# Four small moves in a tuned attention-plus-MLP kernel: last output part in another buffer, one of w_out's four sums by an adding transfer, the verdict in the second batch, x's differences a pair sooner

## The chip, the cores and the metric

The kernel runs on one core of a Trainium2 chip. The metric is the device time of that core in microseconds (us). Every execution quoted here, of every kernel, was in the undisturbed (fast) state: one core alone, at a mean granted TensorE clock (the share of full speed that the chip granted) of 0.992 to 0.999. Times inside a trace count from the start of its span. The span is shorter than the device time of the same execution (895.2 against 897.08 us in the profiled run of the kernel before). In the lines of the profiler, PE is TensorE, DVE VectorE, ACT ScalarE and POOL GpSimd; SPq and ACTq are transfers issued by SyncE and ScalarE; L with a number is a line of the kernel; "issue" is time in which nothing that the profile shows was waited for.

## The reference, cut to what matters

```python
# attention: B=4, H=8, S=768, D=64; proj has 6 columns
mask   = bucket(q) == bucket(k)                 # sign bits of q @ proj, k @ proj
scores = where(mask, q @ k.T / 8, -1e9)
attn   = softmax(scores) @ v                    # float32
x      = attn.transpose(0, 2, 1, 3).reshape(3072, 512)
# MLP: w_in 512 x 2048, w_out 2048 x 512, alpha one value per hidden unit
h      = x @ w_in
g      = maximum(h, 0) + alpha * minimum(h, 0)
out    = g @ w_out                              # float32
```

## The kernel before

First come sixteen pairs of heads (some 340 us), then the MLP in four batches. In each batch eight blocks f_0 to f_7 form g from x and w_in, and seven blocks z form the output. Both layers use a scheme of seven block products in place of eight, so that sums and differences of blocks of x, g and the weights must be made beside the matmuls, most of them by VectorE. A block of the first layer takes TensorE 9.03 us.

Four places are touched.

**w_out's sums.** The second layer needs four combinations of the quarters of w_out. They are made once, in the f blocks of the first batch, in eight pieces n = 0 to 7: GpSimd's queue loads a piece (four planes of 128x256, 512 KB), VectorE makes four sums in place, and GpSimd's queue stores the piece. Two pieces share one tile wo. The wo tiles and the weight tiles wl of the second layer share one buffer of two slots:

```python
def load_w2(b, n):                     # weights of the second layer
    t = late[0].tile([P, NI, 2 * H2], F32, name=f"wl{b}_{n}", tag="wl")      # same two slots
    m = SIDES[ORDER[n]][0]
    nc.sync.dma_start(t, w_out_r[m] if m < 3 else w_out_s[(2, 0, 3, 1)[m - 3]])
    ...
def load_out(n):
    if n % 2 == 0:
        w_o[n] = late[0].tile([P, 2, 4, DM // 2], F32, name=f"wo{n}", tag="wl")
    nc.gpsimd.dma_start(w_o[n - n % 2][:, n % 2], w_out_r[:, :, n].rearrange("m p d -> p m d"))

def sum_out(n):
    w = w_o[n - n % 2][:, n % 2]
    for to, x, op, y in ((2, 3, ALU.add, 2), (3, 0, ALU.subtract, 3), (0, 2, ALU.subtract, 0), (1, 1, ALU.subtract, 0)):
        do(DVE.tensor_tensor(w[:, to], w[:, x], w[:, y], op=op))
    nc.gpsimd.dma_start(w_out_s[:, :, n].rearrange("m p d -> p m d"), w)
...
# j is the number of the block
for n_out in [(), (0,), (1,), (2, 3), (4,), (5, 6), (7,)][j] if j < 7 else ():
    sum_out(n_out)
for n_out in [(1,), (2, 3), (4,), (5, 6), (7,)][j] if j < 5 else ():
    load_out(n_out)
```

So the slot goes from hand to hand: pieces 4 and 5 may be loaded when the stores of 0 and 1 have landed, pieces 6 and 7 when those of 2 and 3 have, the first weight tile wl when those of 4 and 5 have. `do(...)` pins an instruction to the program's order on its engine. The transfers of load_out and sum_out are not pinned, so the scheduler chooses their order on GpSimd's queue.

**The last output tile.** Its two copies by VectorE go into a tile of the ring "o", whose older slot is still being stored:

```python
def turn_last(n):
    ...
    o = late[0].tile([P, 2, P, 2], F32, name=f"o_{p}", tag="o")
    ...
    do(DVE.tensor_copy(o[:, :, :, 0], ps))                                    # tx
    do(ACT.copy(o2.rearrange("p f i -> p i f"), ps2))                         # ty
    nc.scalar.dma_start(dst[:, 2], o2.rearrange("p f i -> p (f i)"))
    do(DVE.tensor_copy(o[:, :, :, 1], cells("tz", [(0, 1), (1, 1)])))
    nc.sync.dma_start(dst[:, :2], o.rearrange("p t f i -> p t (f i)"))        # the last store
```

**The verdict.** In the fifth f block of the first batch, three reductions over saved magnitudes (`largest`), a transposition by TensorE and nine tiny VectorE instructions (`verdict`) set a flag that tells whether the fast path was admissible. **x's differences.** Four subtractions of 128x768 make the combinations of x for the first batch, after pairs 12 to 15.

## Time and profile before

| | before |
|---|---|
| median of 3 runs | 895.83 us (895.3 to 896.73) |
| span of the profiled run | 895.2 us |
| TensorE busy | 883.6 us (99%) |
| VectorE busy | 756.2 us (84%) |
| idle of TensorE after its start, before its last transposition | 1.7 us in the three longest waits |
| from the start of the last transposition (tz, 886.50) to the end of the span | 8.7 us |

TensorE is the bound, and the idle time is all there is to win: the prediction below shows its waits and the end. The middle of the first batch: this is GpSimd's timeline there (start, duration, engine, source line, operation, tiles, count; in brackets how long the engine had stood idle and what released it); L957 are the loads, L964 the stores:

```profile
375.02 1.50 POOL L957 DMA_DIRECT2D wo<-w_out_r  x2 [5.26 <-DMA w_out_s<-wo]
378.04 0.76 POOL L964 DMA_DIRECT2D w_out_s<-wo  x1 [1.52 <-DVE wo L963]
379.75 0.76 POOL L964 DMA_DIRECT2D w_out_s<-wo  x1 [0.96 <-DVE wo L963]
387.71 1.50 POOL L957 DMA_DIRECT2D wo<-w_out_r  x2 [7.21 <-DMA w_out_s<-wo]
...
396.91 0.76 POOL L964 DMA_DIRECT2D w_out_s<-wo  x1 [6.95 <-DVE wo L963]
```

These are loads 4 and 5, stores 2 and 3, loads 6 and 7, and store 5. Both load pairs wait for stores, the stores wait only for VectorE's sums. The corresponding lines of VectorE's timeline show the eight additions of pieces 5 and 6 without any wait, and the first sum of the second layer (ws) with a short one:

```profile
394.81 3.51 DVE L963 TENSOR_TENSOR wo<-wo 128x256 f32<-128x256 f32 x8
...
409.10 0.69 DVE L979 TENSOR_TENSOR ws<-wl 128x512 f32<-128x512 f32 x1 [0.40 <-DMA wl<-w_out_r]
```

### The profile page before, as it was taken

The numbers are of one execution on the slowest core, as the hardware profiler recorded it, in microseconds if no ns is written. First come the engines' busy times: TensorE is split into PE (matmuls) and PEld (weight loads), VectorE is DVE, ScalarE is ACT, GpSimd is POOL, SyncE is SP. The second block draws the span as 40 slices with busy tenths as digits, with TensorE's granted clock in tenths as the row PEclk, the third lists the DMA queues.
The fourth block names the chain that finished last, engine by engine and source line by source line (L and its number), as shares of the span: only waits on it lengthen the run. The fifth ranks groups of instructions, "written<-read, shape, count | busy, mean of one in ns | idle before, by whom it ended". The sixth has DMA issues, their size and how long they took to land.

```text
span 895.2 us, 15372 instructions
## 1 busy us (share of the span) xinstructions
PE 883.6 (99%) x5886; PEld 595.2 (66%) x5886; DVE 756.2 (84%) x1266; ACT 407.2 (45%) x726; POOL 46.2 (5%) x109
## 2 busy tenths in 40 slices
PE   9999999999999999999999999999999999999996
PEld 5544445555555445557997557997557997557996
DVE  5888998989989997899898678988668988668985
ACT  6888888888888862222112222112222112222111
POOL 0000000100100001210000000000000000000000
PEclk9999999999999999999999999999999999999999
DMA  8565586686796726587334434333425242520241
GB/s 224 139 169 136 160 233 165 173 240 194 205 284 177 231 61 218 174 287 284 137 106 131 140 123 153 131 122 104 167 101 177 102 152 83 174 96 0 95 159 57
DMA packets 124978, 140.17 MB, mean 157 GB/s; under 512 B 77776, under 2 KB 109024, under 8 KB 121312
## 3 DMA queue, kind: packets, MB, share of 16 engines
q1 hardware_dynamic: 116368, 123.90, 43.9%
q0 software_dynamic: 6384, 14.29, 6.5%
q10 hardware_dynamic: 2144, 0.92, 0.4%
q8 instruction: 48, 0.79, 0.3%
q14 instruction: 34, 0.28, 0.1%
HBM read 104.87 MB, written 28.31 MB: 149 GB/s over the span
## 4 chain that ended last, share of the span: by engine, by line
PE 90%; DVE 4%; DMA 3%; issue 2%; ACT 1%; SPq 1%; POOL 0%; DVEq 0%; ACTq 0%; POOLq 0%
PE sc L734 17%; PE av L770 13%; PE f_0a L870 2%; PE z_5a L870 2%; PE z_6a L870 2%; PE z_3a L870 2%; PE f_1a L870 2%; PE f_2a L870 2%; PE z_7a L870 2%; PE z_2a L870 2%; PE f_3a L870 2%; PE z_4a L870 2%; PE z_1a L870 2%; PE f_5a L870 2%; PE f_7a L870 2%; PE f_4a L870 2%
## 5 line engine op out<-in xcount | busy, mean ns | idle before, releaser
L737 ACT ACTIVATE pt<-sc 128x768 f32<-128x768 f32 x192 | 154.9, 812 | 38.4 <-PE sc L734 37.9
L734 PE MATMUL sc<-qT,kT 64*128 64x384 f32 x768 | 155.2, 483 | 0.0
L770 PE MATMUL av<-pt,vn 128*32 128x385 f32 (+1 forms) x1536 | 127.4, 487 | 0.0
L770 PEld LDWEIGHTS av<-pt,vn 128*32 128x32 f32 x1536 | 48.9, 109 | 70.9 <-issue 70.0
L734 PEld LDWEIGHTS sc<-qT,kT 64*128 64x128 f32 x768 | 68.2, 188 | 39.5 <-issue 39.3
L923 DVE TENSOR_TENSOR g<-g,g 128x384 f32<-128x384 f32 x128 | 68.4, 555 | 2.2
L734 PE MATMUL sc<-qb,kb 64*128 64x384 bf16 x384 | 63.3, 324 | 0.3 <-DVE kb L719 0.2
L987 DVE TENSOR_TENSOR gs<-g,gs 128x768 f32<-128x768 f32 x56 | 53.3, 952 | 1.0
L987 DVE TENSOR_TENSOR gs<-g 128x768 f32<-128x768 f32 x56 | 53.3, 952 | 0.0
L979 DVE TENSOR_TENSOR ws<-wl 128x512 f32<-128x512 f32 x56 | 38.5, 688 | 17.4 <-DMA wl<-w_out_s 15.9
L919 DVE SCALAR_TENSOR_TENSOR g<-h,alpha 128x384 f32<-128x384 f32 x32 | 19.7, 616 | 26.1 <-ACT h L912 26.1
L734 PEld LDWEIGHTS <-kb 64*128 64x128 bf16 x384 | 19.0, 94 | 27.7 <-issue 4.3
L745 DVE TENSOR_TENSOR accp<-pt,pt 128x1536 f32<-128x1536 f32 x16 | 28.1, 1758 | 10.5 <-ACT pt L737 10.5
L712 ACT ACTIVATE qb<-hs,hb 32x384 bf16<-32x384 f32 x60 | 34.4, 573 | 1.1 <-PE hs L704 0.2
L752 DVE TENSOR_TENSOR accd<-accd,pt 128x1536 f32<-128x1536 f32 x16 | 28.1, 1759 | 1.7
L751 DVE TENSOR_TENSOR accd<-pt,pt 128x1536 f32<-128x1536 f32 x16 | 28.0, 1752 | 0.0
L759 DVE TENSOR_TENSOR accd<-accd,accp 128x1536 f32<-128x1536 f32 x16 | 28.0, 1748 | 0.0
L723 ACT ACTIVATE kb<-hs,hb 64x384 bf16<-64x384 f32 (+1 forms) x45 | 26.0, 577 | 0.6
L870 PE MATMUL f_0a<-x,wi 128*128 128x384 f32 x64 | 23.5, 490 | 0.0
L870 PE MATMUL f_5a<-x,wi 128*128 128x384 f32 x64 | 23.3, 487 | 0.0
L870 PE MATMUL f_7a<-x,wi 128*128 128x384 f32 x64 | 23.3, 487 | 0.0
L870 PE MATMUL f_2a<-x,wi 128*128 128x384 f32 x64 | 23.3, 487 | 0.0
(351 smaller groups left out, 1776.8 us busy)
## 6 DMA issues: line engine op xcount, KB each, us to landing
wi<-w_in_s SPq DMA_DIRECT2D x32, 896.0 KB, 4.7
wl<-w_out_s SPq DMA_DIRECT2D x16, 1024.0 KB, 4.8
wl<-w_out_r SPq DMA_DIRECT2D x12, 1024.0 KB, 4.8
raw<-in_moe_w_out_dram SPq DMA_DIRECT2D x16, 512.0 KB, 4.6
raw<-in_moe_w_in_dram SPq DMA_DIRECT2D x16, 512.0 KB, 4.3
w_in_s<-wsi SPq DMA_DIRECT2D x16, 448.0 KB, 5.5
vn<-in_v_dram SPq DMA_DIRECT2D x16, 384.0 KB, 4.5
x_s<-x SPq DMA_DIRECT2D x16, 384.0 KB, 4.3
```

Source lines behind the costliest of these rows:

```text
L712: do(ACT.activation(bits["q", pi][D * s : D * s + 32, cols], ps["q"][c : c + 32, 0 if engine is DVE else half, :CW], AF.Sign, bias=hb[c : ...
L734: do(PE.matmul(sc[:, s, :CW], what["k", pi][r, ks], what["q", pi][r, qs], start=first, stop=not first,))
L737: do(ACT.activation(pts[kc][:, g, :, :CW], sc[:, :, :CW], AF.Exp, scale=SCALE / DOWN))
L745: do(DVE.tensor_tensor(accp[pi], p(0), p(1), op=ALU.add))
L751: do(DVE.tensor_tensor(accd[pi], p(3), p(4), op=ALU.add))
L752: do(DVE.tensor_tensor(accd[pi], accd[pi], p(5), op=ALU.add))
L759: do(DVE.tensor_tensor(accd[pi], accd[pi], accp[pi], op=ALU.add))
L770: do(PE.matmul(av[pi][D * s + t : D * s + t + 32, g, :w], nat["v", pi][:, s, kc * D + t : kc * D + t + 32], pts[kc][:, g, s, :w], start=(k ...
L870: do(PE.matmul(self.ps[bank], self.left(left, k), self.right(right, k), start=start and k == 0, stop=k == self.nk - 1, skip_group_check=no ...
L923: do(DVE.tensor_tensor(new_g(b, to)[:, i], g_m[b, x][:, i], g_m[b, y][:, i], op=ALU.subtract))
L979: do(DVE.tensor_tensor(t, w2[b, n, x], w2[b, n, y], op=op))
L987: do(DVE.tensor_tensor(t, g2[b, n, x], g2[b, n, y], op=ALU.subtract))
```

## The change

It moves the last output tile into a buffer that has long been free. It lets the transfer that brings plane 3 of each piece of w_out a second time add it onto plane 2 on the way, so that VectorE makes three sums in place of four. It moves the verdict to the second batch, in which no sums of w_out are made. It makes x's differences after pairs 11, 12, 13 and 15.

```diff
         if n % 2 == 0:
             w_o[n] = late[0].tile([P, 2, 4, DM // 2], F32, name=f"wo{n}", tag="wl")
-        nc.gpsimd.dma_start(w_o[n - n % 2][:, n % 2], w_out_r[:, :, n].rearrange("m p d -> p m d"))
+        w = w_o[n - n % 2][:, n % 2]
+        nc.gpsimd.dma_start(w, w_out_r[:, :, n].rearrange("m p d -> p m d"))
+        nc.gpsimd.dma_start(w[:, 2], w_out_r[3, :, n], accum_op=ALU.add)
@@
-        for to, x, op, y in ((2, 3, ALU.add, 2), (3, 0, ALU.subtract, 3), (0, 2, ALU.subtract, 0), (1, 1, ALU.subtract, 0)):
+        for to, x, op, y in ((3, 0, ALU.subtract, 3), (0, 2, ALU.subtract, 0), (1, 1, ALU.subtract, 0)):
@@
-        o = late[0].tile([P, 2, P, 2], F32, name=f"o_{p}", tag="o")
+
+        o = late[0].tile([P, 2, P, 2], F32, name=f"o_{p}", tag="ws3")
@@
-            load_x(0, *{9: (0,), 10: (1, 3), 12: (2,)}[pi])
-        if pi >= 12:
-            sum_x(0, pi - 12, DVE)
+            load_x(0, *{9: (0,), 10: (2, 3), 12: (1,)}[pi])
+        if 11 <= pi < 14 or pi == 15:
+            sum_x(0, min(pi - 11, 3), DVE)
@@
-        if j == 4:
+        if (b, what, n) == (1, "1", 1):
             largest()
@@
-        if j == 4:
+        if (b, what, n) == (1, "1", 3):
             verdict()
```

## The prediction

> **What bounds the kernel now.** I read the busy table first, then TensorE's waits, then the chain of waits at the end and around the largest holes, and last the timelines there. The busy table settles the scale:
>
> ```profile
> PE 883.6 (99%) x5886; PEld 595.2 (66%) x5886; DVE 756.2 (84%) x1266; ACT 407.2 (45%) x726; POOL 46.2 (5%) x109
> ```
>
> TensorE is busy for 883.6 of a span of 895.2 us. The change adds or removes no matmul, so all it can touch is the remaining 11.6 us. TensorE's waits divide the inner part of it:
>
> ```profile
> PE nil L514 <- DVE hb L518: 1.2, 1, 1.2
> PE z_2c L870 <- DVE m L1008: 0.8, 1, 0.8
> PE sm L784 <- DVE accd L759: 0.6, 1, 0.6
> PE vd L1087 <- DVE top L1083: 0.3, 1, 0.3
> ```
>
> The first is the start. The other three are the verdict at 383 us, the second product of the first batch at 425 us, and the sums of pair 14 at 319 us: 1.7 us together. The rest, 8.3 us, lies after the last transposition of TensorE (886.94 us). The chain of waits and the timeline of the end show:
>
> ```profile
> 884.93 0.43 SPq L1040
> 885.36 0.04 issue
> 885.40 3.00 DMA out_dram<-o
> ```
>
> ```profile
> 888.44 0.43 DVE L1068 COPY o<-tx 128x256 f32<-128x256 f32 x1 [2.00 <-DMA out_dram<-o]
> 888.78 0.41 DVE L1071 COPY o<-tz 128x256 f32<-128x256 f32 x1
> 889.23 0.40 SPq L1072 DMA_DIRECT2D out_dram<-o  x1
> ```
>
> The last copy is ready for its input at 886.4 us, but its tile o is a slot whose previous contents are still being stored by twelve small transfers. VectorE sits 2.00 us for that. The last store follows at 889.23 us and lands 3.1 us later.
>
> The second place is the middle of the first batch, where w_out's sums pass through a tile that shares its slots (wl) with the weights of the second layer. The chain of waits there:
>
> ```profile
> 396.91 7.00 DMA w_out_s<-wo
> ...
> 404.25 4.83 DMA wl<-w_out_r
> 409.07 0.02 issue
> 409.10 0.70 DVE ws L979
> ```
>
> So the first weight load of the second layer waits for a store of w_out's sums (issued 396.91, landed 403.91), and VectorE cannot go on before 409.10. From there VectorE's timeline is gapless to 425.05, when it releases the bank for z_2c. TensorE's start there is thus the landing plus 16.0 us, however early TensorE comes.
>
> **What the Trainium skill says.** "DMA: Bandwidth & Descriptors", section "SWDGE vs HWDGE vs iDMA", says an accumulating DMA must be issued by GpSimd, so the eight new ones share POOL's queue with the loads and stores of the same tiles. Section "Anatomy of one DMA — SWDGE (gpsimd) path" says DMA engines do not wait on semaphores: the issuing sequencer waits before dispatch. The trace agrees: POOL waits 12.5 us for two stores before it issues loads, and everything behind stands. The same section gives 2.0 us + bytes/436e3; for 512 KB that is an estimate of 3.2 us. The trace shows a median of 7.2 us for the loads (3.8 us the quickest), because section "Issuing engines are not separate DMA queues" of that page applies: all queues interleave on the same 16 engines, and each 9.03 us block brings an 896 KB weight load. "PSUM — Partial Sum Buffer", section "Engine vs sequencer instructions", says VectorE's queue is strict FIFO, so a sum that waits for an adding transfer holds all of VectorE's later work.
>
> **The change, part by part.**
>
> Last part to a free place: the second last-store tile moves to ws3, whose older slot was last read a block earlier. The copy then follows VectorE's own m at 886.44: 0.43 us to 886.87. The second copy needs tz, 886.94: about 886.98 to 887.39. The issue is at about 887.42 instead of 889.23, a gain of 1.8 us. By then the 128 KB store on ScalarE's queue, issued at 886.95, is in flight, so I count 1.7 us.
>
> Verdict later: TensorE's f_4a starts at 381.79 and four matmuls take 1.29, so f_5a could start at 383.08; it starts at 383.67. The loss is 0.59 us, and VectorE spends about 0.25 + 1.4 us there while it is already late. In the second batch there are no sums of w_out, and the reductions are two blocks ahead of the transposition: I charge 0.1 us. But the 0.59 us does not count by itself: TensorE meets VectorE at z_2c anyway, so it only makes that wait longer unless VectorE or the load is earlier too.
>
> x's differences: four of 0.95 us, all still there, now after pairs 11, 12, 13, 15 instead of 12, 13, 14, 15. Pair 14's wait of 0.6 us comes out of VectorE's own run from 304.53 to 319.13, which begins when exp frees it (a gap of 0.35 us before accp). Pair 13 ends with one difference in both kernels, so this wait stays. After pair 11 VectorE had 1.7 us idle, which takes the extra 0.95. Value: 0.
>
> One sum by an adding transfer: eight additions of 0.43 us leave VectorE, 3.4 us, in blocks of the first layer where it is 86 to 96% busy. In exchange POOL's order becomes load, adding transfer (after the load's landing), store. The adding transfers of the attention part move 384 KB and land after 4.3 us at the quickest; for 128 KB I estimate 3 us from that. The compiled order puts the store of sum 2 behind adding transfers 4 and 5, the store of sum 4 behind adding transfer 6, and that of sum 5 behind 7. I followed the clock with durations of before. Store 1 goes at 368.2, lands about 374; loads 4 and 5 at 374.2 and 375.0, land about 378 and 379.5 to 383; stores 2 and 3 leave at 380.5 to 384 (before 378.04 and 379.75), land 387.5 to 391; loads 6 and 7 land 394 to 399 (before 394.6 and 396.1). Adding transfer 6 leaves at 394 to 397 and lands at 397 to 401. VectorE wants it at about 395.6, in front of six g's that TensorE needs for f_7b at 404. So VectorE, which finished these sums at 398.24 before, finishes them between 397 and 402. Store 5 leaves at 397 to 400 (before 396.91); wl lands at 408.5 to 412.5 (before 409.07). Whichever is later moves the 16.0 us run: minus 1 to plus 4 us, with the middle at plus 0.6.
>
> Sum: 895.8 − 1.7 (end) + 0.1 (verdict in the second batch) + 0.6 (middle of the first batch) + 0 (x) = 894.8.
>
> **The rivals.** First, everything works: no adding transfer is late, the load of wl lands a little sooner because VectorE reaches sum 5 some 2 us earlier, and the 1.9 us that TensorE loses between 383 and 425 (0.59, and 1.3 around z_2) go. That makes 895.8 − 1.7 − 1.9 = 892.2. For it speaks that VectorE's lateness is real; against it that the load waits for a transfer, not for an addition.
>
> Second, POOL's queue becomes the bound: one weight load of 896 KB cuts into load 5, as before, when it took 9.1 us, every later step comes 4 us later, and VectorE stands at sum 6. It makes 895.8 − 1.7 + 4.5 = 898.6. For it speaks the order on POOL and the long landings; against it that each store is only half as late by the time of the next, since the weight loads pace them.
>
> Third, the last store is not sooner, because it meets the stores still in flight (384 KB issued at 885.38, landed 888.2). Then 1 us of the 1.7 is lost: 895.8. Against it: its data begin only at about 888.9 if the delay of before (889.23 to 890) or somewhat more holds, when those are done.
>
> **Range and chances.** I give the first rival 0.35, the middle course 0.4, the second 0.25, and lean slightly to the good side: 894.7, with 892.2 to 898.6 for 8 in 10. 2% is 17.9 us, more than the whole idle time of TensorE, so faster by 2% is all but impossible; slower by 2% would need a stall of 20 us, which only a transfer chain far longer than any seen here would make.
>
> **What would show it.** In the changed profile: the copy o<-tx at about 886.5 with no wait for a store, the last issue at about 887.4; no wait of TensorE for top; the wait of sm unchanged at 0.6; VectorE's wait for an adding transfer at the sums of the sixth block; and ws of the first batch at 408 to 413, with the wait of z_2c moved with it. If there is no wait for the adding transfers and ws begins before 408, I was too dark; if VectorE stands at several sums, too bright. Waits of TensorE in the later batches would mean that I missed something.

## The result, and the profile after

The kernel became slower: a median of 902.09 us (901.35 to 903.17, six runs) against 896.37 us (895.3 to 896.93, six runs of the kernel before, the three early ones among them). The ratio is 1.0066, with a 95% interval of 1.0054 to 1.0079. Here and below a ratio is that of the mean times of fast runs of the same rounds (the figures come out when the first, profiled, execution of each kernel is left out), so it is not quite the ratio of the medians. The time lies above the predicted range (892.2 to 898.6), though inside 2%.

VectorE lost 3.3 us of work (752.9 us busy in place of 756.2), and the span still grew by 5.0 us, to 900.2. TensorE's waits in the profile after (us in total, times, longest) say where:

```profile
PE f_7b L870 <- DVE f_6p L915: 5.1, 1, 5.1
PE nil L514 <- DVE hb L518: 1.2, 1, 1.2
PE z_2c L870 <- DVE m L1010: 0.8, 1, 0.8
PE sm L784 <- DVE accd L759: 0.6, 1, 0.6
```

The wait for the verdict (vd) is gone, those of sm and z_2c are as they were, and a new one of 5.1 us stands at the first batch's last f block. TensorE's timeline shows it, and a second effect behind it:

```profile
401.87 1.45 PE L870 MATMUL f_6a<-x,wi 128*128 128x384 f32 x4
408.41 2.93 PE L870 MATMUL f_7b<-x,wi 128*128 128x384 f32 x4 [5.09 <-DVE f_6p L915]
411.13 1.82 PE L870 MATMUL f_7c<-x,wi 128*128 128x384 f32 x4
```

After the hole the same four matmuls take 2.93 and 1.82 us in place of 1.45: the granted clock was 0.72 from 408 to 414 us. That is what the Trainium skill warns of in "TensorE: Matmul & The Clock Gate", section "HAM oscillation — how this bites in real kernels", for idle gaps of TensorE over some 3.4 us, and the trace agrees. Here it cost nothing by itself: VectorE was the later of the two until z_2c, and its timeline shows no wait for TensorE between 404.36 and there.

TensorE waited because VectorE did. VectorE's timeline after, where L965 are the sums of w_out (three per piece now):

```profile
393.44 1.34 DVE L965 TENSOR_TENSOR wo<-wo 128x256 f32<-128x256 f32 x3
400.97 0.43 DVE L965 TENSOR_TENSOR wo<-wo 128x256 f32<-128x256 f32 x1 [6.19 <-DMA wo<-w_out_r]
404.36 0.88 DVE L965 TENSOR_TENSOR wo<-wo 128x256 f32<-128x256 f32 x2 [2.96 <-DMA wo<-w_out_r]
...
415.07 0.68 DVE L981 TENSOR_TENSOR ws<-wl 128x512 f32<-128x512 f32 x1
```

Piece 5 is summed at 393.44. Piece 6 then makes VectorE wait 6.19 us for its load (its first remaining sum needs planes 0 and 3 only) and another 2.96 us for its adding transfer. In the kernel before, piece 6 had landed by the time it was wanted. The addition f_6p, which empties the bank that f_7b writes, comes behind it. And ws begins at 415.07 in place of 409.10, 6.0 us later, without waiting for wl itself.

GpSimd's timeline after tells why piece 6 came so late (L958 loads, L959 adding transfers, L966 stores):

```profile
374.58 1.50 POOL L958 DMA_DIRECT2D wo<-w_out_r  x2 [5.80 <-DMA w_out_s<-wo]
379.49 0.91 POOL L959 DMA_DIRECT2D wo<-w_out_r  x1 [3.41 <-DMA wo<-w_out_r]
384.54 0.87 POOL L959 DMA_DIRECT2D wo<-w_out_r  x1 [4.13 <-DMA wo<-w_out_r]
385.10 1.88 POOL L966 DMA_DIRECT2D w_out_s<-wo  x2
394.61 1.50 POOL L958 DMA_DIRECT2D wo<-w_out_r  x2 [7.63 <-DMA w_out_s<-wo]
401.14 0.91 POOL L959 DMA_DIRECT2D wo<-w_out_r  x1 [5.03 <-DMA wo<-w_out_r]
...
403.34 1.17 POOL L966 DMA_DIRECT2D w_out_s<-wo  x1
```

Loads 4 and 5 start as early as before (374.58). But stores 2 and 3, which left at 378.04 and 379.75 before, now stand behind adding transfers 4 and 5, and adding transfer 5 waits until load 5 has landed, at about 384.2. So these stores leave at 385.10, loads 6 and 7 at 394.61 in place of 387.71, and add 6 can leave only at 401.14, when load 6 has landed. It lands at 404.27. That is the chain of waits of this stretch: load, landing, add, landing, store, landing, next load. Each link was there before except the adding one, which puts one more landing into each turn.

There is a second limit close behind the first. Store 5, which frees the slot of wl, leaves at 403.34 in place of 396.91. The first load of wl leaves SyncE's queue after that:

```profile
408.86 0.32 SPq L947 DMA_DIRECT2D wl<-w_out_r  x1
```

It took 5.6 us, so it landed at about 414.5, only 0.6 us before VectorE, itself late, asked for it.

From z_2c on both traces run alike: z_2c starts 5.95 us later than before, tz 6.03 us later (892.53 against 886.50), and the span ends 5.0 us later. So the new end is 1.0 us shorter than the old one. Its timeline:

```profile
892.39 0.42 DVE L1071 COPY o<-tx 128x256 f32<-128x256 f32 x1
...
893.00 0.42 DVE L1074 COPY o<-tz 128x256 f32<-128x256 f32 x1 [0.20 <-PE tz L1056]
894.27 0.39 SPq L1075 DMA_DIRECT2D out_dram<-o  x1
```

Neither copy waits for a store any more, as intended. But the last store leaves 0.85 us after its last copy ended (893.42). The waits of SyncE name what held it:

```profile
SPq L1075 <- DMA out_dram<-o: 2.0, 1, 2.0
```

It waits for another store, one that doesn't touch its tile. The compiled program counts the landings of all transfers of SyncE and ScalarE, loads too, on a set of eight semaphores, taken in turn (this is read from the built program, not from a trace). The turn of the last store falls on the semaphore of ScalarE's 384 KB store (issued at 891.40, landed 2.8 us later, at 894.2). In the kernel before that same wait existed, but the copy's own wait for the buffer (to 888.40) hid it.

### The profile page after: what moved, and what is told of

Same layout as the page of the kernel before. It is cut to its first block, busy times and chain, and to the rows that moved or that the text cites.

```text
span 900.2 us, 15377 instructions
## 1 busy us (share of the span) xinstructions
PE 884.9 (98%) x5886; PEld 595.3 (66%) x5886; DVE 752.9 (84%) x1258; ACT 407.1 (45%) x726; POOL 53.6 (6%) x117
## 4 chain that ended last, share of the span: by engine, by line
PE 51%; DMA 3%; issue 3%; DVE 3%; POOL 1%; POOLq 0%; DVEq 0%
PE z_4a L870 2%; PE z_7a L870 2%; PE z_3a L870 2%; PE z_6a L870 2%; PE z_5a L870 2%; PE z_2a L870 2%; DMA wo<-w_out_r 2%; PE z_1a L870 2%; PE f_4a L870 2%; PE f_7a L870 2%; PE f_6a L870 2%; PE f_5a L870 2%; PE f_3a L870 2%; PE f_2a L870 2%; PE f_1a L870 2%
## 5 line engine op out<-in xcount | busy, mean ns | idle before, releaser
L870 PE MATMUL f_1a<-x,wi 128*128 128x384 f32 x64 | 23.3, 486 | 0.0
L870 PE MATMUL f_3a<-x,wi 128*128 128x384 f32 x64 | 23.3, 486 | 0.0
```

The costliest lines, as they stand in the source:

```text
L870: do(PE.matmul(self.ps[bank], self.left(left, k), self.right(right, k), start=start and k == 0, stop=k == self.nk - 1, skip_group_check=no ...
```

## The experiments

Theory at the start: the whole loss comes from the adding transfers, through their place in GpSimd's order (T1); the end gained about 1.0 us, and the rest of the predicted 1.7 is the shared semaphore; verdict and x are worth half a microsecond or nothing. Rivals: the adding transfer's own way is too long in any order (R1); another part of the change, or several together, cause the loss (R2); the last store meets others in flight whatever it waits for (R3). All twelve results were correct. The runs came in three sets of rounds, each with its own executions of the kernel before: e1, e2, e3 and e7; e4, e6, e8 and e9; e5, e10, e11 and e12. In the table, "before" is the median of the kernel before in the same rounds. Each trace is of one execution: those of e1, e2, e8 and e11 are the slowest of their kernels (896.55, 903.64, 902.02 and 904.80 us), those of e6, e7 and e12 the fastest.

| run | what it is | median (range) | before | ratio (95%) |
|---|---|---|---|---|
| e1_tail | before + end | 895.18 (894.71–896.55) | 896.31 | 0.9985 (0.9972–0.9998) |
| e2_add | before + adding transfers | 902.06 (898.51–903.64) | 896.31 | 1.0056 (1.0040–1.0071) |
| e3_no_add | after − adding transfers | 895.13 (894.21–896.03) | 896.31 | 0.9985 (0.9972–0.9998) |
| e7_lane | e1 + other semaphore | 895.33 (894.69–895.76) | 896.31 | 0.9988 (0.9975–1.0001) |
| e4_verdict | before + verdict | 896.34 (895.34–896.67) | 896.67 | 0.9993 (0.9979–1.0007) |
| e6_add4 | after, adds for pieces 0–3 only | 894.64 (894.21–895.23) | 896.67 | 0.9977 (0.9964–0.9991) |
| e8_pinned | after, GpSimd's order by hand | 900.30 (899.72–902.02) | 896.67 | 1.0040 (1.0025–1.0056) |
| e9_sooner | e3 + piece 5 a block sooner | 894.46 (893.75–894.88) | 896.67 | 0.9972 (0.9959–0.9986) |
| e5_x | before + x | 896.35 (896.00–896.77) | 896.10 | 1.0003 (0.9990–1.0016) |
| e10_not6 | after, no add for piece 6 | 899.98 (895.46–901.28) | 896.10 | 1.0028 (1.0007–1.0050) |
| e11_later | after, pieces 6 and 7 summed together later | 901.65 (896.13–904.80) | 896.10 | 1.0049 (1.0030–1.0067) |
| e12_both | e9 + e7's edit | 894.18 (893.38–894.44) | 896.10 | 0.9979 (0.9966–0.9992) |

### The parts one by one

**e2_add**: only the adding transfers, onto the kernel before.

```diff
+        nc.gpsimd.dma_start(w[:, 2], w_out_r[3, :, n], accum_op=ALU.add)
-        for to, x, op, y in ((2, 3, ALU.add, 2), (3, 0, ...), (0, 2, ...), (1, 1, ...)):
+        for to, x, op, y in ((3, 0, ...), (0, 2, ...), (1, 1, ...)):
```

> The kernel before with the adding transfers alone. Theory: they alone cause the loss, and the verdict's old place makes it no better: TensorE waits about 4 to 6 us for f_7b, the time rises by 6 to 7 us, ratio 1.007 to 1.008. Rival: the loss comes from the other parts or from their meeting, and the adding transfers alone cost less than 3 us, ratio under 1.0035.

It was 1.0056 times the kernel before, with the same wait of 5.1 us at f_7b and 9.1 us of VectorE's time lost in two waits for piece 6. The adding transfers alone bring at least most of the loss, so R2 is out as its main cause. Whether they cost more beside the other three parts stays open: 1.0056 times e3's 0.9985 below is 1.0041, against 1.0066 for all four parts, a difference at the edge of the intervals.

**e3_no_add**: the change without them.

```diff
-        nc.gpsimd.dma_start(w[:, 2], w_out_r[3, :, n], accum_op=ALU.add)
-        for to, x, op, y in ((3, 0, ...), (0, 2, ...), (1, 1, ...)):
+        for to, x, op, y in ((2, 3, ALU.add, 2), (3, 0, ...), (0, 2, ...), (1, 1, ...)):
```

> The changed kernel with the adding transfers taken back, the other three parts kept. Theory: the wait for f_7b is gone, the end gains 1.0 us, the verdict's 0.6 us and part of z_2c's 1.3 us are gained too: 1.3 to 2.9 us faster than before, ratio 0.9968 to 0.9985. Rival (verdict or x does harm): 0 to 5 us slower than before.

The other three parts together gave 0.9985, about 1.3 us. The new wait at f_7b was gone, and so was the one for the verdict; z_2c still waited 0.8 us. VectorE's timeline shows what became of the room that the verdict left:

```profile
408.33 0.69 DVE L979 TENSOR_TENSOR ws<-wl 128x512 f32<-128x512 f32 x1 [0.84 <-DMA wl<-w_out_r]
```

VectorE arrives sooner and then waits longer for wl, 0.84 us in place of 0.40. But this wait differs between executions in which the verdict stands in its old place: 1.16 us in e1, none shown in e5 and e7. That VectorE is ready sooner is steady: its sums of piece 7 begin 34.44 us after the second store of w_out's sums in e3 and e4, 35.24 or 35.25 us in the kernel before, e1, e5 and e7. What that is worth depends on when wl lands.

**e4_verdict**: the verdict alone.

```diff
-        if j == 4:
+        if (b, what, n) == (1, "1", 1):
             largest()
-        if j == 4:
+        if (b, what, n) == (1, "1", 3):
             verdict()
```

> The kernel before with the verdict in the second batch alone. Theory: TensorE's wait for top goes (0.6 us), but it meets the same 16 us run of VectorE, which starts with the landing of the weights: z_2c is at most 0.5 us sooner, ratio 0.9993 to 1.0. Rival: VectorE's 1.7 us pass on to everything after, 1.3 to 1.9 us faster, ratio 0.998 to 0.9985.

0.9993, not told apart from 1. The wait of 0.3 us was gone; z_2c waited 0.8 us, one of 0.5 us stood at z_1a (as in e1, with the verdict in its old place), and VectorE stood 1.00 us at ws for wl. In this execution the load set the start of ws, so the time saved ahead of it was only waited away.

**e5_x**: x's differences alone.

```diff
-            load_x(0, *{9: (0,), 10: (1, 3), 12: (2,)}[pi])
-        if pi >= 12:
-            sum_x(0, pi - 12, DVE)
+            load_x(0, *{9: (0,), 10: (2, 3), 12: (1,)}[pi])
+        if 11 <= pi < 14 or pi == 15:
+            sum_x(0, min(pi - 11, 3), DVE)
```

> The kernel before with x's differences a pair sooner alone. Theory: worth nothing, TensorE's wait for pair 14's sums stays at 0.6 us, ratio 0.999 to 1.001. Rival: VectorE's extra 0.95 us after pair 11 makes TensorE wait at pair 12, or the missing one after pair 14 takes the wait of 0.6 us away: a difference of 0.6 us or more, ratio under 0.9993 or over 1.0007 with a changed wait in the trace.

1.0003, and the wait of sm was 0.6 us as before: no gain is shown.

### The end

**e1_tail**: the other buffer alone.

```diff
-        o = late[0].tile([P, 2, P, 2], F32, name=f"o_{p}", tag="o")
+        o = late[0].tile([P, 2, P, 2], F32, name=f"o_{p}", tag="ws3")
```

> The kernel before with the last tile moved to ws3 alone. My theory from the changed kernel's profile: the copy no longer waits, but the last store still waits for the semaphore that it shares with the 384 KB store on ScalarE's queue (there the store was issued 0.85 us after its copy), so the gain is 1.0 us, ratio 0.9989; the last store is issued about 1.3 us after the last transposition (2.3 before). The rival, which is the prediction's step: 1.7 to 1.8 us, ratio 0.998. A third: no gain at all, the stores only queue up later.

The time fell to 0.9985. The last store left at 888.80, 1.77 us after tz began (887.03); before it was 2.73 us (889.23 − 886.50). From the start of tz to the end of the span it is 7.8 us in place of 8.7. So the end is worth about 1.0 us, and SyncE again waited for another store, 2.1 us.

**e7_lane**: on top of it, three of the twelve small stores of the tile before go to GpSimd's queue, so that the turn of the last store falls on another semaphore.

```diff
-                    nc.sync.dma_start(
+                    (nc.gpsimd if (b, p, a) == (B - 1, 3, 3) else nc.sync).dma_start(
```

> The kernel before with the last tile in ws3, and three of the twelve 32 KB stores ahead of it given to GpSimd's queue, so that the last store's semaphore is one of another, long finished, store. Theory: the last store is issued right after its copy, 0.8 us sooner than in the run with ws3 alone, and the gain over before is 1.8 us, ratio 0.998. Rival: the store is held by traffic and not by the semaphore: issued sooner but landing no sooner, no more than the 1.0 us of ws3 alone.

Now the last store left right behind its copy, 0.93 us after the start of tz:

```profile
885.90 0.42 DVE L1072 COPY o<-tz 128x256 f32<-128x256 f32 x1 [0.20 <-PE tz L1054]
886.35 0.39 SPq L1073 DMA_DIRECT2D out_dram<-o  x1
```

and SyncE's wait for a store was replaced by one for VectorE's copy. The shared semaphore is thereby shown to be the cause of the 0.85 us. But the store, now beside the 384 KB one, took 4.0 us to land in place of 3.3, and from tz to the end of the span it is 7.5 us against 7.8. The timed runs show no difference between e7 and e1. R3 is partly right: most of what the semaphore held back was lost again to the slower landing. That the stores in flight made it slower is likely, but no run isolates it.

### Why the adding transfers cost what they do

**e8_pinned**: GpSimd's order fixed by hand, with all stores ahead of the adding transfers that they don't depend on: stores 2 and 3 before adds 4 and 5, stores 4 and 5 before adds 6 and 7.

```diff
-        nc.gpsimd.dma_start(w, w_out_r[:, :, n].rearrange("m p d -> p m d"))
-        nc.gpsimd.dma_start(w[:, 2], w_out_r[3, :, n], accum_op=ALU.add)
+        do(POOL.dma_start(w, w_out_r[:, :, n].rearrange("m p d -> p m d")))
+    def add_out(n):
+        w = w_o[n - n % 2][:, n % 2]
+        do(POOL.dma_start(w[:, 2], w_out_r[3, :, n], accum_op=ALU.add))
@@  (the stores pinned likewise; loads and adds 0 to 3 at the start, then, by block)
+            1: ((sum_out, 0),), 2: ((sum_out, 1), (load_out, 4), (load_out, 5)),
+            3: ((sum_out, 2), (sum_out, 3), (add_out, 4), (add_out, 5), (load_out, 6), (load_out, 7)),
+            4: ((sum_out, 4),), 5: ((sum_out, 5), (add_out, 6), (add_out, 7), (sum_out, 6)), 6: ((sum_out, 7),),
```

> The changed kernel with all eight adding transfers, but POOL's order fixed by hand so that the stores of w_out's sums go ahead of the adding transfers that wait for later loads. Theory (the loss is POOL's order: stores stand behind adding transfers, so later loads and adding transfers come late): VectorE's wait at the sums of the sixth block falls from 9.2 to about 3 us, TensorE's wait for f_7b of 5.1 us is gone, and the time is within 1 us of the run without adding transfers, ratio to before 0.998 to 1.001. Rival (the adding transfer's own way, load, landing, add, landing, is too long whatever the order): f_7b still waits 3 us or more, ratio 1.003 or more.

Theory T1 fell as an account of the whole loss. The order did what it should: loads 6 and 7 left at 387.58 as before, store 5 at 396.16, wl at 403.85. But VectorE stood at piece 6 all the same, this time for the adding transfer alone:

```profile
404.24 0.89 DVE L969 TENSOR_TENSOR wo<-wo 128x256 f32<-128x256 f32 x2 [8.04 <-DMA wo<-w_out_r]
```

In the chain of waits (start, duration, what) the two adding transfers that matter, 4 and 6, took twice what I had estimated and more:

```profile
379.62 8.00 DMA wo<-w_out_r
```

```profile
396.16 0.75 POOL w_out_s L970
396.91 7.23 DMA wo<-w_out_r
```

Each is issued right behind a 512 KB store on the same queue and beside a weight load of 896 KB. In the kernel after, where the adds come ahead of the stores, the eight landed in 3.1 to 5.6 us (median 4.4); here in 3.3 to 8.0 us (median 7.0). So an add ahead of the stores delays the slots, and adds 4 and 6 behind them were themselves late. That the place behind a store made them slow is not shown: adds 0 to 3 of the same run, with no store ahead of them, took 3.3 to 7.7 us. TensorE waited 4.4 us at f_7b, and the time was 1.0040, less than the 1.0066 of the kernel after; so the order seems to matter for a part, though the intervals just touch. R1 holds for the two orders tried, not for "any order": load 6, issued at 387.58, landed 6.7 us later at 394.3, but my order puts add 6 behind store 5, which waits for VectorE's sums of piece 5, and so it left only at 396.91. An order with stores 2 and 3 ahead of adds 4 and 5, and add 6 ahead of store 5, was not tried.

**e6_add4**: adding transfers for pieces 0 to 3 only, whose loads wait for no store; four sums for pieces 4 to 7.

```diff
+        if (n < 4):
             nc.gpsimd.dma_start(w[:, 2], w_out_r[3, :, n], accum_op=ALU.add)
```

> The changed kernel with adding transfers only for the first four of the eight sums, whose loads are issued before VectorE needs them. Theory: no wait for f_7b, as without adding transfers, ratio 0.997 to 0.9995. Rival (each adding transfer costs its share): half the loss stays, about 3 us, ratio 1.002 or more.

0.9977. No wait at f_7b, ws at 407.14 without any wait, z_2c waits 0.5 us. An adding transfer with time to spare is harmless; the loss sits in pieces 4 to 7, whose slots are handed on.

**e10_not6**: all adding transfers but that of piece 6, the one VectorE stood for.

```diff
+        if n != 6:
             nc.gpsimd.dma_start(w[:, 2], w_out_r[3, :, n], accum_op=ALU.add)
```

> The changed kernel with adding transfers for all sums but number 6. In the changed kernel VectorE stood 6.2 us at sum 6 for the load and 3.0 us for the adding transfer. Theory: both causes count, the late load (its slot is freed by stores that stand behind adding transfers 4 and 5 on POOL) and the adding transfer itself; without the latter the load's 6 us stay, VectorE is held until about 401, TensorE waits 1.5 to 3 us for f_7b instead of 5.1, ratio to before 1.002 to 1.004. Rival (only the adding transfer's own way counts): no wait for f_7b, ratio under 1.0.

VectorE now waited only 3.75 us at piece 6, for its load, and TensorE 0.2 us at f_7b. In its place came a wait of TensorE for the weights of the second layer:

```profile
PE z_1a L870 <- DMA wl<-w_out_r: 3.4, 1, 3.4
```

Store 5 stood behind add 7 and left only at 402.36 (396.91 before), so wl landed late. The six runs fall into two groups: two at 895.5 us and four from 899.88 to 901.28 us; the trace is one of the four (900.07 us).

**e11_later**: all adding transfers, but pieces 6 and 7 are summed together a block later, so that VectorE doesn't ask for piece 6 before it is there.

```diff
-        for n_out in [(), (0,), (1,), (2, 3), (4,), (5, 6), (7,)][j] if j < 7 else ():
+        for n_out in [(), (0,), (1,), (2, 3), (4,), (5,), (6, 7)][j] if j < 7 else ():
```

> The changed kernel with sum 6 taken one block later, beside sum 7; all eight adding transfers stay. Theory (the cost is VectorE's wait at sum 6, which is asked for before its transfers can be done): the wait for f_7b goes, VectorE waits some 1.5 us at sum 6 and up to 3 at sum 7 a block later, ws starts at about 411 instead of 415, ratio 0.999 to 1.002. Rival (the chain of transfers itself is the limit): the second layer's first weights come as late as VectorE did, ratio above 1.004.

My theory fell here too: I had hoped that VectorE's wait was all there was. f_7b no longer waited, but TensorE's waits had a longer one:

```profile
PE z_1a L870 <- DMA wl<-w_out_r: 7.6, 1, 7.6
```

and GpSimd's timeline shows the way to it:

```profile
403.90 0.92 POOL L959 DMA_DIRECT2D wo<-w_out_r  x1 [6.54 <-DMA wo<-w_out_r]
404.77 0.84 POOL L966 DMA_DIRECT2D w_out_s<-wo  x1
405.53 0.97 POOL L959 DMA_DIRECT2D wo<-w_out_r  x1
406.11 1.17 POOL L966 DMA_DIRECT2D w_out_s<-wo  x1
```

Add 6, store 4, add 7, store 5: the store that frees the slot of wl leaves 9.2 us later than before (406.11 against 396.91), and wl's load leaves at 411.67. This is the second limit. In this execution TensorE's clock was then 0.50 from 414 to 423 us and z_2c no longer waited for VectorE, so the low clock may have added to the 904.80 us; the six runs range from 896.13 us up. e8 lifts the second and not the first, e10 and e11 (nearly) lift the first and not the second; e6, which drops adds 4 to 7, lifts both.

### A version that beats both kernels

**e9_sooner**: e3 (no adding transfers), with piece 5 summed and stored one block sooner, so that the slot of wl comes free sooner.

```diff
-        for n_out in [(), (0,), (1,), (2, 3), (4,), (5, 6), (7,)][j] if j < 7 else ():
+        for n_out in [(), (0,), (1,), (2, 3), (4, 5), (6,), (7,)][j] if j < 7 else ():
```

> The changed kernel without adding transfers, and with sum 5 taken in the fifth block instead of the sixth, so that its store, which frees the slot of the second layer's first weights, leaves some 8 us sooner. Theory (what is left of z_2c's wait hangs on that slot): the weights land long before VectorE asks for them, VectorE's wait for them (0.84 us without adding transfers) is gone, ws starts about 1 us sooner against the end of the attention part, z_2c waits less than 0.3 us, 0.5 to 1.3 us faster than without adding transfers, ratio to before 0.9965 to 0.9985. Rival: VectorE itself is the limit there, ws starts no sooner, ratio as without adding transfers, 0.9985.

Both stores left together at 388.40 (store 5: 396.91 before), and VectorE found wl landed:

```profile
407.22 0.69 DVE L979 TENSOR_TENSOR ws<-wl 128x512 f32<-128x512 f32 x1
```

z_2c no longer waited; of TensorE's waits only those of the start and the attention part were left (1.2, 0.6 and 0.2 us). The median was 894.46 us, 0.9972. The trace shows the wait gone; the times alone don't tell e9 apart from e3 (0.9985, in other rounds; the intervals overlap).

**e12_both**: e9 with e7's three stores on GpSimd's queue.

```diff
-                    nc.sync.dma_start(
+                    (nc.gpsimd if (b, p, a) == (B - 1, 3, 3) else nc.sync).dma_start(
```

> The best version in sight: no adding transfers, verdict later, x sooner, last tile in ws3, sum 5 a block sooner, and the last store's semaphore freed as before by giving three small stores to GpSimd. Theory: the 0.8 us by which the last store is issued sooner is half lost again to a slower landing (4.0 us against 3.3 in the two runs of the end), so 0.2 to 0.5 us faster than with sum 5 sooner alone: ratio to before 0.9964 to 0.9972. Rival: no difference to that run.

894.18 us, 0.9979. It has the lowest median of all, but isn't told apart from e9 (their rounds had different medians of the kernel before, 896.10 and 896.67). Either beats the kernel before and the kernel after.

## Why the prediction was wrong

**The end.** The mechanism was right (the copies wait for no store), the size was not: the term "1.8 us, so I count 1.7" measured 1.0. The step that failed is "The issue is at about 887.42": I looked only at what the store reads, not at what its completion semaphore had been used for last. The issue came 0.85 us after the copy. The third rival, that the last store meets stores in flight, took back the rest where the semaphore was out of the way (e7).

**The verdict and x.** As predicted, neither is told apart from no effect: 0.9993 and 1.0003. The argument that the 0.59 us "does not count by itself" fits e4's trace, where VectorE waited 1.00 us for wl; it would not bind in an execution in which wl lands early, as in e5 and e7.

**The adding transfers.** This is the failed step: "Adding transfer 6 leaves at 394 to 397 and lands at 397 to 401", and with it "minus 1 to plus 4 us, with the middle at plus 0.6". The runs put these in its place:

| step | predicted | measured in the profile after |
|---|---|---|
| loads 4 and 5 leave | 374.2, 375.0 | 374.58, 375.3 |
| load 5 lands | 379.5 to 383 | about 384.2 |
| stores 2 and 3 leave | 380.5 to 384 | 385.10, 385.9 |
| stores 2 and 3 have landed, so that loads 6 and 7 can leave | 387.5 to 391 | about 394.1; they leave at 394.61 |
| loads 6 and 7 land | 394 to 399 | about 400.8, 402.3 |
| add 6 leaves | 394 to 397 | 401.14 |
| add 6 lands | 397 to 401 | 404.27 |
| store 5 leaves | 397 to 400 | 403.34 |
| wl lands | 408.5 to 412.5 | about 414.5 |
| ws (before 409.10) | −1 to +4 us | +6.0 us |

The estimate of 3 us for an adding transfer was good for the one at hand (3.1 us), though short of the median of the eight (4.4 us). What failed was load 5 and stores 2 and 3: load 5 took 8.9 us, as the 9.1 us that the second rival quoted from the kernel before, and the two stores took 9.0 us from the first issue to the second landing (7.7 and 8.2 us each) where I had given them 7. I knew the long values and let the chain run on medians; but in a chain in which each link waits for the landing of the one ahead, the lateness of the links adds up, and the ends of my range were middling values added. As an estimate: with the long values of the kernel before (9.1 us for load 5, 8.1 us for a store, stores 0.75 us apart) the same working gives some 393 for loads 6 and 7. The second rival describes what happened, the weight load cutting into load 5 and VectorE standing at piece 6; I gave it 0.25 and 4.5 us. It was 6.0 us in the middle, and all six runs lie above my range. The claim against it, that "each store is only half as late by the time of the next, since the weight loads pace them", is wrong: against the kernel before, store 2 was 7.1 us late (385.10 against 378.04), loads 6 and 7 were 6.9 us late and store 5 still 6.4 us.

The sum with the measured terms, 895.8 − 1.0 + 6.0 and nothing for verdict and x, is 900.8 us. The median is 902.09; 0.5 us of the rest is the kernel before itself, whose median in six runs was 896.37. The last 0.8 us lies between the executions: the traced one of the kernel before (897.08 us) was 0.7 us slower than its median, the traced one of the kernel after (902.00 us) was at its median, and the terms are read from these two. Some kernels with late adding transfers scatter far more (e2 by 5.1 us, e11 by 8.7 us, e10 in two groups) than those without any (at most 1.9 us for e1, e3, e5, e9 and e12, 2.7 us for the kernel before in one set of rounds), though the kernel after itself by only 1.8 us. That the scatter comes from whether an 896 KB load happens to cut in is my reading of it; no run here shows it.

The eight additions that left VectorE, 8 × 0.43 = 3.4 us, bought nothing: they stood ahead of waits for transfers. What was short in this stretch was not VectorE's time but the two slots.

## What to carry to other kernels

Before moving work from an engine into a transfer, ask whether the buffer it works in is handed on: an adding transfer must wait for the landing of its load and adds a landing of its own, and in a chain with two slots that delay reaches the next load, the next store and whatever takes the slot afterwards. Where the data lie ready for long, it is harmless (e6); where the slot is the bound, freeing it a block sooner without any cheaper sum (e9) removed VectorE's wait for the transfer that takes the slot next, while the eight cheaper sums cost some 5 us (e2). When an instruction is freed from one wait, look for the next one it has, the semaphore of its completion included, and when a chain of landings is predicted, add up the long values of its links, not the medians.

## What the Trainium skill lacked or had wrong

- "DMA: Bandwidth & Descriptors", section "Anatomy of one DMA — SWDGE (gpsimd) path": its fit of 2.0 us + bytes/436e3 makes an estimate of 2.3 us for the 128 KB of an adding transfer. The eight of the kernel after landed in 3.1 to 5.6 us (median 4.4), those of e8 in 3.3 to 8.0 us (median 7.0), the slowest right behind a 512 KB store of the same queue and beside an 896 KB load. The page gives no figure for an accumulating transfer, nor for one behind earlier transfers of its queue.
- The same page, section "Why a DMA increments its semaphore by 16 and not by 1", asks for one semaphore per in-flight slot. I found on no page what a small set of semaphores taken in turn costs: a store then waits for an unrelated one, 0.85 us at the end of the kernel after (copy ended at 893.42, store issued at 894.27, the unrelated 384 KB store landed at 894.2).
